# A lightweight convolution and a SwiGLU block: half of one DMA placing issued later on ScalarE, two values ahead of two taps on VectorE

## The chip, the cores and the metric

One core of a Trainium2 chip runs the whole program. Its engines are TensorE (PE in the profile, with its weight loads as PEld), VectorE (DVE), ScalarE (ACT), GpSimd (POOL) and SyncE (SP, which here only issues DMAs). Each engine works off its own list of instructions in the order in which the program gave them, and waits on semaphores for the others. The metric is the device time of one execution in microseconds (us), lower is better.

## What is computed

The reference, cut to what matters (B = 8, S = 4096, D = 192, 8 heads, 7 taps, 32768 tokens in all, inner width 1536, all in fp32):

```python
w = softmax(weight, axis=-1)                     # 8 heads x 7 taps
x_pad = concatenate([zeros((B, 6, D)), x], axis=1)
out = einsum('hk,bskhg->bshg', w, x_unf)         # causal convolution, 7 taps, weights by head
x = out.reshape(B * S, D)

rms = sqrt(mean(x * x, axis=-1) + 1e-06)
xn = x / rms * rms_g
g = xn @ w_gate
val = xn @ w_val
return (g * sigmoid(g) * val) @ w_out
```

## The kernel before, in words

The tokens are cut into 32 pieces of 1,024, which the code calls pairs (two groups of 512 tokens each). For every pair the kernel

- loads x with its halo into `xh` (`load_heads`, issue L144, eight DMAs on SP),
- convolves it into `y` (`tap` L421 in whole, or `part_tap` in three parts of 512 columns: the first tap on ACT into a PSUM bank at L437, the other six on DVE at L445, the last of which writes `y`),
- normalises: `square` on ACT (L461), `reduce` on DVE (L472 to L474), `factor` on POOL (L478 to L484), `spread` on DVE (L491), `scale` on POOL (L499), which leaves `yn`,
- turns the result over through DRAM: `place` writes `yn` to the scratch `xd` (L635, one DMA for each of eight heads), `fetch` reads it back as `xb`, features on partitions (L648, four DMAs; `fetch_part`, L661, in later pairs),
- multiplies with the gate and value weights, and then with the output weights.

From the second pair on the products go by a scheme with fewer multiplications (Strassen-like): it needs sums of operands, which DVE makes at L670 from `xb` into `xc` (`x_sum`), and sums of weights, which POOL makes at L346 and L350 (`w_sums`) and L825 (`out_sums`). Its products on PE are L759, its output products L899.

The first pair is plain: products at L1011 (24 groups of six, in an upper and a lower half of the array), a silu on ACT at L1021 and the value product on DVE at L1028 for each group, then the output products at L1051 (`outer`), cleared from PSUM by ACT at L1059 and DVE at L1063 and stored at L1068. While it runs, the weights are converted (L287 to L319, L298 to L302, L310, L311), the second pair (p = 1) is convolved and normalised, and the third (p = 2) is begun, with its x loaded early.

There are eight PSUM banks, ps0 to ps3 for one half and ps4 to ps7 for the other. A list of free banks is kept for each half while the program is written. The part taps of pair 2 take ps1, ps5 and ps3; the second half of `outer` for the first pair starts in ps1, once the part taps have given it back.

The order is written by hand. For the first pair the string `START` has a letter for each step, and each letter calls the next step of one generator: `p` a group of products, `s` its silu, `v` its value product, `c` a tap of pair 1, `w` four sums of weights, `i` and `o` steps of conversion, `n` a step of normalising, `t` the placing of pair 1. The list `LATER` puts more steps at places (numbers on a line of dues, `put(at, ...)`), and the code behind it puts the part taps, the fetch and the sums the same way. Steps with smaller numbers are emitted first:

```python
put(c + 240 + 700 * (j // 2), functools.partial(part_tap, 2, 0, j))
later(place(2), c + 2450)
```

with `base` = 4 x 1509 and `c` = `base + 200`. So the first two L437 of pair 2 (j = 0, 1) stand at `base + 440`, the fetch of pair 1 at `base + 450`, the third L437 (j = 2) at `base + 1140`. The step `t` stands at `base + 60` in `LATER`; in this kernel it issues all eight DMAs of L635, the odd heads on ACT, the even ones on SP. From pair 2 on `place` issues all eight on SP.

Of the kernel before, what the change touches and what calls it, by code (L numbers as in the profile page):

```python
# [19 lines left out]
def kernel(  # L20
# [10 lines left out]
    nc = tc.nc  # L31
# [3 lines left out]
    H, K = weight.shape  # L35
# [201 lines left out]
    def load_out(i):  # L237
# [28 lines left out]
        out=taps[:], in0=w_sb[:], in1=stat[:].to_broadcast([P, H, K]), op=ALU.subtract  # L266
# [7 lines left out]
        out=taps[:], in0=taps[:], in1=ssum[:].to_broadcast([P, H, K]), op=ALU.mult  # L274
# [84 lines left out]
    def convert_in(u):  # L359

        t = raw.pop(("in", u))
        dst = wf[u][:, 0:9, :].rearrange("p (k f) n -> p k (f n)", k=KP)
        step = P if u == 0 else NF * P
        parts = [slice(i, i + step) for i in range(0, NF * P, step)]
        return [
            convert(t[:, :, c, :], exp_i[:, :, c], mf_i[:, :, c], dst[:, :, c], rg_sb)
            for c in parts
        ]

    def convert_out(i):  # L370
        dst = wo_sb[:, i * PF : (i + 1) * PF, :]
        yield from convert(raw.pop(("out", i)), *cvt[i % 3], dst)
# [131 lines left out]
    def conv(p):  # L504

        for k in range(K):
            tap(p, k)
            if k == K - 1:
                load(p + 1)
            yield  # L510

    def norm(p):
        for part in (square, reduce, factor, spread, scale):
            part(p)
            yield
# [107 lines left out]
    def place(p):  # L623

        if p >= PAIRS:
            return
        y = yn.pop(p)  # L630
        xd = scr[p] = dram.tile([D, PT], F32, name="xd")
        to = xd[:].rearrange("(h a) (b t) -> h b a t", a=GS, t=TB)
        for h in range(H):
            q = nc.scalar if p == 1 and h % 2 else nc.sync
            q.dma_start(out=to[h], in_=y[h::H])  # L635
        yield

    def x_op(i):
        return xb[:, i // KP, i % KP, :] if i < 2 * KP else xc[:, i - 2 * KP, :]
# [36 lines left out]
    def bank(half, i):  # L676
        return ps[half * 4 + i]
# [6 lines left out]
    def pick(h, full):  # L684

        i = next((i for i in free[h] if ((h, i) in whole) == full), free[h][0])
        free[h].remove(i)
        return i
# [5 lines left out]
    def put(at, do):  # L694
        heapq.heappush(line, (at, next(tick), do))
# [301 lines left out]
    def plain(hts):  # L997


        groups = [(u, g, f) for u in range(NU) for g in (1, 0) for f in range(NF)]  # L1000
        groups[0 : 2 * NF] = [(0, g, f) for f in range(NF) for g in (1, 0)]
        held = {}

        def products():
            for u, g, f in groups:
                if len(hts) <= u:
                    hts.append(big.tile([P, 2, NF, T], F32, name="ht"))
                bks = held[u, g, f] = [free[h].pop(0) for h in range(2)]
                for k in range(KP):
                    for h in range(2):  # L1010
                        nc.tensor.matmul(  # L1011
                            out=bank(h, bks[h])[:], lhsT=wf[u][HALF[h], k * NF + f, :],
                            rhs=xb[HALF[h], g, k, :], start=(k == 0), stop=(k == KP - 1),
                            skip_group_check=True,
                        )
                yield

        def silus():
            for i in groups:
                sg = tiles.pop(0)  # L1020
                nc.scalar.activation(out=sg[:], in_=bank(0, held[i][0])[:], func=AF.Silu)  # L1021
                held[i].append(sg)
                yield

        def values():
            for u, g, f in groups:
                *bks, sg = held.pop((u, g, f))
                nc.vector.tensor_tensor(  # L1028
                    out=hts[u][:, g, f, :], in0=bank(1, bks[1])[:], in1=sg[:], op=ALU.mult
                )  # L1030
                tiles.append(sg)
                for h in range(2):
                    free[h].append(bks[h])
                yield

        return products(), silus(), values()
# [7 lines left out]
    def outer(p, hts, base):  # L1044


        def mm(h, bks, g, j, w, f, first, give=None):
            if first:
                bks[h] = free[h].pop(0) if first is True else pick(h, False)
                whole.discard((h, bks[h]))  # L1050
            nc.tensor.matmul(  # L1051
                out=bank(h, bks[h])[:, w : w + D],
                lhsT=hts[f // NF][HALF[h], g, f % NF, j * P : (j + 1) * P],
                rhs=wo_sb[HALF[h], f, :], start=(f == 0 and w == 0),
                stop=(f == FC - 1), skip_group_check=True,
            )

        def low(dst, bks, n):
            nc.scalar.copy(out=dst, in_=bank(0, bks[0])[:, 0:n])  # L1059
            free[0].append(bks[0])  # L1060

        def upp(dst, bks, n):
            nc.vector.tensor_tensor(out=dst, in0=bank(1, bks[1])[:, 0:n], in1=dst, op=ALU.add)  # L1063
            free[1].append(bks[1])

        def store(g, o_sb, lo=0, hi=T // P):
            r = p * PT + g * T
            nc.sync.dma_start(  # L1068
                out=out[r + lo * P : r + hi * P, :].rearrange("(j p) d -> p j d", p=P),
                in_=o_sb[:, lo:hi, :],  # L1070
            )

        def soon(*a):
            put(base + n * STEP + LAG + OVER + 1, functools.partial(store, *a))

        n = 0

        def mms(bks, g, j, w, fs, first):
            nonlocal n
            for i, f in enumerate(fs):  # L1080
                for h in range(2):
                    at = base + n * STEP + h * LAG
                    put(at, functools.partial(mm, h, bks, g, j, w, f, first if i == 0 else False))
                n += 1

        def evac(dst, bks, w):
            put(base + n * STEP + OVER, functools.partial(low, dst, bks, w))
            put(base + n * STEP + LAG + OVER, functools.partial(upp, dst, bks, w))

        for g in range(2):  # L1090
            o_sb = outs.tile([P, T // P, D], F32, name="o_sb")
            if g == 0:

                bks = [{}, {}]
                for fs in (range(0, FC // 2), range(FC // 2, FC - NF)):
                    for j in range(4):
                        mms(bks[j // 2], g, j, j % 2 * D, fs, j % 2 == 0 and fs[0] == 0)
                for j in range(4):
                    mms(bks[j // 2], g, j, j % 2 * D, range(FC - NF, FC), False)
                    if j % 2:  # L1100
                        dst = o_sb[:, j - 1 : j + 1, :].rearrange("p j d -> p (j d)")
                        evac(dst, bks[j // 2], 2 * D)
            else:
                for j in range(0, 2 if p == PAIRS - 1 else 4, 2):
                    b = {}
                    mms(b, g, j, 0, range(FC), "used" if j else True)
                    mms(b, g, j + 1, D, range(FC), False)
                    evac(o_sb[:, j : j + 2, :].rearrange("p j d -> p (j d)"), b, 2 * D)

                if p == PAIRS - 1:  # L1110
                    soon(g, o_sb, 0, 2)
                    for j in range(2, 4):
                        b = {}
                        mms(b, g, j, 0, range(FC), True)
                        evac(o_sb[:, j, :], b, D)
                        soon(g, o_sb, j, j + 1)
                    continue
            soon(g, o_sb)
# [7 lines left out]
    def done(it):  # L1126
# [7 lines left out]


    START = (
        "XxxxxxXDdDdDTDdadTbTaTfbTakTakTakTkbkKkKkKkbkbfpoffpfsicpsvivOpsipisvicpsvpvwsicwpvs"
        "iwpvscwpsiwvpisvicpsvovpwispvswcipvwspsiwOvpsiwvipsvvpswopsvcpsvOnovoOpsonvOpsnoOvnopsoO"
    )
    LATER = (  # L1140
        (30, "s"), (35, "v"), (40, "O"), (45, "v"), (50, "O"), (55, "n"), (60, "t"),
# [9 lines left out]
    for i in range(2, NO):  # L1151
        load_out(i)
    hts = []
    p, sl, v = plain(hts)
    pieces = {
        **cross(),
        **dict(zip("abf", convert_in(0))),
        "i": itertools.chain(*[convert_in(u)[0] for u in range(1, NU)]),
        "o": itertools.chain(*[convert_out(i) for i in range(0, NO, 2)]),
        "O": itertools.chain(*[convert_out(i) for i in range(1, NO, 2)]),  # L1160
        "c": conv(1), "n": norm(1), "t": place(1),
        "p": p, "s": sl, "v": v,
        "w": itertools.chain(*[w_sums(u) for u in range(NU)]),
# [15 lines left out]

    base = NU * SPAN  # L1180
    put(base - 1, lambda: outer(0, hts, base))
    put(base + 450, functools.partial(fetch, 1))
    both.extend(flat[:, i * T : (i + 1) * T] for i in range(NK - len(both)))
    rest.extend(t[:, 2, :] for t in tl6)
# [69 lines left out]
```

## Time and profile before

| what | value |
|---|---|
| device time, three runs | 2611.20, 2612.31, 2613.34 us, median 2612.31 |
| the profiled execution | 2610.37 us, its span 2608.6 us |
| granted TensorE clock over the span | 0.998 |
| PE busy | 2572.9 us, 99% |
| DVE, POOL, ACT busy | 89%, 84%, 59% |
| PE's share of the chain that ended last | 96% |
| L759, products of the later pairs | 62% of that chain |
| L899, output products of the later pairs | 33% |
| L1011 and L1051, the first pair | 1% each |

The span runs from the first to the last instruction; the execution's own time is 1.8 us more. The page divides the span into 40 slices of 65 us; in those a stall of a few us can't be seen, so stages are read from timelines over short stretches. A timeline line has the start, the length, the engine, the line, what is written and read, and how many instructions are merged in it; a bracket at its end has the idle time of the engine ahead of it and what ended it.

### The profile page before, as it was taken

Reading aid. Unit: us, or ns where it says so; the run is one execution under the profiler, and the core shown is the slowest. Engines: PE = TensorE matmul, PEld = TensorE weight load, DVE = VectorE, ACT = ScalarE, POOL = GpSimd, SP = SyncE. Lnnn points to the kernel's source line nnn. Section 1 sums busy time; section 2 is a strip of 40 time slices with the busy share of each in tenths; the row PEclk is TensorE's granted clock in tenths of the full one; section 3 lists DMA queues with packets and bytes.
Section 4 is the critical chain, followed back from the end, with each engine's and each line's share of the span. In section 5 each row is a group of like instructions: output and inputs, shape, how many; then the busy total and the mean of one; then the engine's idle time right before and its main releaser. Section 6 shows DMA issues by size and latency. Waiting matters only on the chain.

```text
span 2608.6 us, 60634 instructions
## 1 busy us (share of the span) xinstructions
PE 2572.9 (99%) x23794; PEld 1756.9 (67%) x23794; DVE 2309.3 (89%) x3679; ACT 1545.0 (59%) x2812; POOL 2189.0 (84%) x1786
## 2 busy tenths in 40 slices
PE   6899999999999999999999999999999999999999
PEld 3586667666676666676666766666766666766666
DVE  8888989889989889898899898898898898988975
ACT  5365556765556655557655566555576555676554
POOL 3878889888898888898888988888988888988877
PEclk9999999999999999999999999999999999999999
DMA  6222331223322223313233222233132333222210
GB/s 144 51 39 56 63 54 41 54 41 63 63 45 49 44 52 63 60 38 58 34 63 63 47 48 45 51 63 63 40 55 34 62 63 54 41 54 41 50 44 13
DMA packets 512602, 137.35 MB, mean 53 GB/s; under 512 B 484284, under 2 KB 486844, under 8 KB 512189
## 3 DMA queue, kind: packets, MB, share of 16 engines
q1 hardware_dynamic: 509068, 132.80, 26.9%
q8 instruction: 186, 3.05, 0.5%
q10 hardware_dynamic: 3248, 0.69, 0.1%
q14 instruction: 100, 0.82, 0.1%
HBM read 83.87 MB, written 49.55 MB: 51 GB/s over the span
## 4 chain that ended last, share of the span: by engine, by line
PE 96%; DVE 2%; issue 0%; DMA 0%; ACT 0%; POOL 0%; ACTq 0%; DVEq 0%; SPq 0%; POOLq 0%
PE ps L759 62%; PE ps L899 33%; PE ps L1011 1%; PE ps L1051 1%; DMA x<-in_x_dram 0%; DVE ht L1028 0%; DVE xc L304 0%; DVE y L406 0%; DVE y L421 0%; DVE ps L445 0%; DVE y L394 0%; DVE wf L319 0%; ACT xb L615 0%; PE ps L595 0%; ACTq L635 0%
## 5 line engine op out<-in xcount | busy, mean ns | idle before, releaser
L759 PE MATMUL ps<-xc,wf 64*128 64x512 f32 x4960 | 1216.6, 591 | 0.0
L759 PEld LDWEIGHTS ps<-xc,wf 64*128 64x128 f32 x4960 | 680.5, 186 | 376.8 <-issue 181.3
L759 PE MATMUL ps<-xb,wf 64*128 64x512 f32 x2480 | 682.3, 591 | 0.0
L708 ACT ACTIVATE tile<-ps 128x512 f32<-128x512 f32 x678 | 391.2, 593 | 389.7 <-PE ps L759 296.1
L708 ACT ACTIVATE tls<-ps 128x512 f32<-128x512 f32 (+1 forms) x562 | 323.4, 589 | 437.9 <-PE ps L759 221.4
L811 POOL TENSOR_TENSOR ht<-ht,tile 128x512 f32<-128x512 f32 x329 | 419.0, 1275 | 144.2 <-ACT tile L804 65.6
L759 PEld LDWEIGHTS ps<-xb,wf 64*128 64x128 f32 x2480 | 354.0, 187 | 183.0 <-issue 96.3
L811 POOL TENSOR_TENSOR ht<-ht,tls 128x512 f32<-128x512 f32 x260 | 330.6, 1274 | 86.2 <-ACT tls L804 40.4
L708 ACT ACTIVATE ps<-ps 128x512 f32<-128x512 f32 (+1 forms) x589 | 336.1, 581 | 88.0 <-PE ps L899 32.6
L927 POOL TENSOR_TENSOR early<-ht 128x512 f32<-128x512 f32 x279 | 354.9, 1277 | 5.1 <-POOL ht L811 0.3
L445 DVE SCALAR_TENSOR_TENSOR ps<-xh,tp,ps 128x512 f32<-128x512 f32 x450 | 320.3, 748 | 10.7 <-ACT ps L437 8.5
L899 PE MATMUL ps<-ht,wo_sb 128*32 128x128 f32 (+2 forms) x5208 | 318.5, 380 | 0.0
L899 PEld LDWEIGHTS ps<-ht,wo_sb 128*32 128x32 f32 x5208 | 233.9, 110 | 81.7 <-POOL ht L811 23.5
L899 PE MATMUL ps<-ht,x 128*32 128x128 f32 (+2 forms) x4464 | 250.7, 379 | 0.0
L791 DVE TENSOR_TENSOR tile<-ps,tile 128x512 f32<-128x512 f32 x349 | 237.4, 683 | 10.4 <-PE ps L759 5.4
L927 POOL TENSOR_TENSOR ht<-ht 128x512 f32<-128x512 f32 x186 | 239.1, 1286 | 4.9
L791 DVE TENSOR_TENSOR ht<-ps,tile 128x512 f32<-128x512 f32 x328 | 222.5, 680 | 5.9 <-ACT tile L708 5.9
L899 PEld LDWEIGHTS ps<-ht,x 128*32 128x32 f32 x4464 | 184.6, 110 | 61.2
L804 ACT ACTIVATE tile<-tile 128x512 f32<-128x512 f32 x349 | 214.5, 625 | 0.0
L791 DVE TENSOR_TENSOR ht<-ps,tls 128x512 f32<-128x512 f32 x292 | 198.9, 681 | 7.1 <-ACT tls L708 3.9
L791 DVE TENSOR_TENSOR tls<-ps,tls 128x512 f32<-128x512 f32 x271 | 184.8, 683 | 16.7 <-PE ps L759 13.3
L899 PE MATMUL ps<-early,x 128*32 128x256 f32 (+2 forms) x3348 | 196.0, 379 | 0.0
(130 smaller groups left out, 3250.8 us busy)
## 6 DMA issues: line engine op xcount, KB each, us to landing
xb<-xd SPq DMA_DIRECT2D x124, 384.0 KB
xd<-yn SPq DMA_DIRECT2D x244, 96.0 KB
xh<-in_x_dram SPq DMA_DIRECT2D x192, 105.0 KB
out_dram<-o_sb SPq DMA_DIRECT2D x122, 96.0 KB
out_dram<-o_sb SPq DMA_DIRECT2D x62, 128.0 KB
xh<-in_x_dram SPq DMA_DIRECT2D x56, 98.4 KB
out_dram<-o_sb SPq DMA_DIRECT2D x122, 32.0 KB
ht<-in_moe_w_gate_dram SPq DMA_DIRECT2D x12, 192.0 KB
```

The source lines that it names most:

```text
L445: nc.vector.scalar_tensor_tensor(out=dst, in0=xk, scalar=w, in1=at, op0=ALU.mult, op1=ALU.add)
L708: nc.scalar.activation(out=dst, in_=src, func=AF.Copy, scale=float(s))
L759: nc.tensor.matmul(out=self.new(v, h, True) if first else self.old(v, h), lhsT=wf[self.u][HALF[h], WAT[i], :], rhs=x_op(XOP[i])[HALF[h]], ...
L791: nc.vector.tensor_tensor(out=self.hv(v) if h else t[:], in0=self.old(v, h), in1=t[:], op=plus(s))
L804: nc.scalar.activation(out=t[:], in_=src[:], func=AF.Silu)
L811: engine[eng].tensor_tensor(out=self.hv(v), in0=src, in1=t[:], op=ALU.mult)
L899: nc.tensor.matmul(out=self.bank(b)[i * Q : (i + 1) * Q, at : at + n], lhsT=left, rhs=cols, start=fresh, stop=True, skip_group_check=True, ...
L927: engine[eng].tensor_tensor(out=dst, in0=a, in1=b, op=op)
L1011: nc.tensor.matmul(out=bank(h, bks[h])[:], lhsT=wf[u][HALF[h], k * NF + f, :], rhs=xb[HALF[h], g, k, :], start=(k == 0), stop=(k == KP - 1 ...
L1051: nc.tensor.matmul(out=bank(h, bks[h])[:, w : w + D], lhsT=hts[f // NF][HALF[h], g, f % NF, j * P : (j + 1) * P], rhs=wo_sb[HALF[h], f, :] ...
```

## The change

Three edits.

1. `place` becomes a generator of two steps for p = 1: the first issues the even heads on SP, the second the odd heads on ACT. For every other pair it stays one step with all heads on SP.
2. The second step is put at `base + 445`: behind the first two L437 of pair 2 (`base + 440`) and ahead of the fetch of pair 1 (`base + 450`). The first step stays at `base + 60`.
3. In `START`, twice, a `v` that stood behind a `c` now stands ahead of it (`wsicw` becomes `wsivcw` with the `v` behind it gone, and the same once more in the next row).

```diff
-        for h in range(H):
-            q = nc.scalar if p == 1 and h % 2 else nc.sync
-            q.dma_start(out=to[h], in_=y[h::H])
-        yield
+        for first in range(2) if p == 1 else (0,):
+            q = nc.scalar if first else nc.sync
+            for h in range(first, H, 2 if p == 1 else 1):
+                q.dma_start(out=to[h], in_=y[h::H])
+            yield
...
     START = (
-        "XxxxxxXDdDdDTDdadTbTaTfbTakTakTakTkbkKkKkKkbkbfpoffpfsicpsvivOpsipisvicpsvpvwsicwpvs"
-        "iwpvscwpsiwvpisvicpsvovpwispvswcipvwspsiwOvpsiwvipsvvpswopsvcpsvOnovoOpsonvOpsnoOvnopsoO"
+        "XxxxxxXDdDdDTDdadTbTaTfbTakTakTakTkbkKkKkKkbkbfpoffpfsicpsvivOpsipisvicpsvpvwsivcwps"
+        "iwpvscwpsiwvpisvivcpsovpwispvswcipvwspsiwOvpsiwvipsvvpswopsvcpsvOnovoOpsonvOpsnoOvnopsoO"
     )
...
     put(base - 1, lambda: outer(0, hts, base))
+    put(base + 445, functools.partial(next, pieces["t"], None))
     put(base + 450, functools.partial(fetch, 1))
```

In the instruction lists this moves the following and nothing else. On ACT, the four issues of L635 go from ahead of the three L437 of pair 2 to between the second and the third. On DVE, a value product L1028 changes places with the tap L421 ahead of it, at two points: those at 59.20 and at 70.37 us in the profile before. The lists of PE, POOL and SP are the same, but for the numbers of the DMA semaphores that some of them wait for.

## The prediction

> **What bounds the kernel now.** I read the page first: PE is busy 99% of the span and holds 96% of the chain that ended last. So an edit is worth only what PE waits, or loses in speed, because of it. The 40 slices show PE below 9 in the first two alone, so I went through 0 to 150 us: the timelines of PE, ACT, DVE, POOL and SP, then a table of stretches for the granted clock.
>
> PE, 100.5 to 142 us (start, us, what; in brackets the idle time before it and its releaser):
>
> ```profile
> 101.10 15.70 PE L1051 MATMUL ps<-wo_sb,ht 64*128 64x192 f32 x183
> 123.57 18.39 PE L1051 MATMUL ps<-wo_sb,ht 64*128 64x192 f32 x195 [6.77 <-DVE y L445]
> 141.64 0.69 PE L759 MATMUL ps<-xc,wf 64*128 64x512 f32 x1
> ```
>
> The largest hole in PE's work, 6.77 us, ends with a tap of pair 2 (L445), which frees ps1. Who holds the taps up, ACT and DVE:
>
> ```profile
> 105.62 0.54 ACT L302 ACTIVATE tls<-tls 128x384 f32<-128x384 uint32 x1
> 111.67 3.59 ACTq L635 DMA_DIRECT2D xd<-yn  x4
> 115.46 1.91 ACT L437 ACTIVATE ps<-xh,tp 128x512 f32<-128x512 f32 x3 [9.30 <-DMA xd<-yn]
> ```
>
> ```profile
> 106.27 1.39 DVE L304 SCALAR_TENSOR_TENSOR xc<-tls,xc 128x384 uint32<-128x384 uint32 x1
> 116.18 6.68 DVE L445 SCALAR_TENSOR_TENSOR ps<-xh,tp,ps 128x512 f32<-128x512 f32 x10 [8.52 <-ACT ps L437]
> 122.77 1.40 DVE L445 SCALAR_TENSOR_TENSOR y<-xh,tp,ps 128x512 f32<-128x512 f32 x2
> 124.09 3.91 DVE L445 SCALAR_TENSOR_TENSOR ps<-xh,tp,ps 128x512 f32<-128x512 f32 x5
> ```
>
> ACT has nothing to do from 106.16 to 111.67: the four issues of L635 stand first and wait for yn. The chain of waits confirms it and names the origin, POOL's scaling at L499:
>
> ```profile
> 108.76 2.87 POOL yn L499
> 111.63 0.36 POOL wf L350
> 111.99 0.27 ACTq L635
> ```
>
> The clock (columns: stretch, length, busy time and count of PE, PEld, DVE, ACT, POOL, PEclk, DMA share, GB/s):
>
> ```profile
> 116.80:123.50 6.70, 0.00 (x0) 0.00 (x0) 6.70 (x12) 0.98 (x2) 6.01 (x14) 0.81 0.61 141
> 123.50:125.50 2.00, 1.93 (x12) 1.93 (x14) 1.97 (x4) 0.00 (x0) 1.84 (x5) 0.50 1.07 214
> 127.50:129.50 2.00, 2.00 (x26) 2.00 (x26) 1.72 (x3) 0.68 (x1) 0.94 (x2) 0.94 0.00 1
> ```
>
> After the hole PE works at half clock until 127.74 (clock record of the trace). Two more small holes lie in the first pair's products, both before DVE's values (L1028):
>
> ```profile
> 61.87 1.13 PE L1011 MATMUL ps<-xb,wf 64*128 64x512 f32 x4 [0.24 <-DVE ht L1028]
> 73.03 1.55 PE L1011 MATMUL ps<-xb,wf 64*128 64x512 f32 x5 [0.22 <-DVE ht L1028]
> ```
>
> **What the Trainium skill says.** "TensorE: Matmul & The Clock Gate", Part 1: after an idle window of about 3.4 us the array falls to half clock, and an equally long busy window restores it. The trace agrees: 0.50 granted from 120.91 (4.1 us into the hole) to 127.74, 6.83 us. The same page, under "Architectural detail", calls ACT and DVE strict first-in first-out; the 9.30 us in which ACT's L437 stands behind the waiting issues is that. "DMA: Bandwidth & Descriptors", "Queues, rings and completion order": on one queue each DMA engine consumes descriptors in ring order. The trace agrees: the x loads (96-byte packets) issued at 221.69, behind output stores (256-byte packets), send their first packet at 222.5, as the stores' last ones leave. "SBUF — State Buffer", "SBUF: two separate sides": DVE and GpSimd share a port pair by an exclusive lock, which a DVE operation with two SBUF inputs takes part in. The taps of L445 have one input in PSUM, and L499 took 2.87 to 2.92 us in all 31 pairs beside a DVE that is 89% busy: no contention seen for this pair of operations.
>
> **Part 1, the placing.** The four DMA issues on ACT go behind the first two of the three L437; they still wait for L499. SP's four, and everything else on SP, POOL and PE, keep their order; only ACT's list changes.
>
> - When can the two L437 run? x of pair 2 (SP's issues from 90.09 to 96.98) has its last packet at 99.77. ps1 and ps5 were last read before 101. ACT is free at 106.16: two of 0.70 us at a pitch of 0.64 end at 107.5.
> - DVE ends its last L304 at 107.66 and then starts the taps, at 107.7 instead of 116.18: 8.5 us earlier. The first y ended 7.34 us after the first tap (123.52 less 116.18); now 115.05. It also needs L499 past (111.63), which it is.
> - The issues stay at 111.67 to 115.26, so the third L437 runs 115.4 to 116.1. The twelve taps end at about 115.7, the last six (4.7 us) at 120.85.
> - PE got to the end of its queue at 116.5. The bank is free at 115.05, so the hole closes. Start to start it was 123.569 - 116.475 = 7.09 where 0.16 is normal: 6.93 us.
> - With no hole the clock stays up. From 123.57 to 127.74 PE started 26 records 0.160 us apart against 0.080 at full clock: 26 x 0.080 = 2.08 us.
>
> **Part 2, two values ahead of taps.** L1028 of 0.68 us goes before a tap of L421 of 2.0 us, at 59.20 and at 70.37. Their silus ended at 53.64 and 64.56, so no new wait. ps5 comes free 1.9 us earlier, both holes vanish. Start to start they show 0.83 and 0.81 us for 0.43, and 0.53 for 0.43 on the next: 0.5 us each, 1.0 in all. The taps follow at once, and the second value stays where it was. Next late are the values at 65.59 and 76.03: they end 0.1 to 0.2 us before PE, now 0.5 to 1.0 ahead, needs their banks. So between 0.7 and 1.0; I take 0.9.
>
> **What is late next.** PE alone would gain 6.93 + 2.08 + 0.9 = 9.9 us at its first L759 (141.64, so 131.7). But that needs an x sum (xc slot 5), and this chain does not move: L499 ends 111.63, the placing lands (last packet 117.78), SP fetches xb:
>
> ```profile
> 118.25 2.60 SPq L648 DMA_DIRECT2D xb<-xd  x4
> 128.87 7.30 SPq L144 DMA_DIRECT2D xh<-in_x_dram  x8
> ```
>
> The last 2,048-byte packet of xb ends at 127.63. DVE starts the sums at 127.7 (in between: square 120.9 to 122.4, L472 to L474 done by 125, so DVE waits for xb). Before, the sums ran 132.58 to 140.56 and slot 5, the seventh, was there 5.44 us after their start: now 133.15. So PE waits 1.5 us at the first L759 (too short for the clock to fall) and starts it 8.5 us earlier. In the old trace three records of L1051 stood mixed into its start; free of them PE is up to 8.9 ahead.
>
> DVE, however, ends its sums at 135.7 and the two L1063 at 136.9; the values it owes PE's first bank (L785, 144.59 before) are due at 135.7. It is late by about 1.2 us, and PE has 0.7 us of room before the same bank's next product: 0.5 back. POOL's L499 and eleven L825 end at 144.9, its first L811 is due at 143.7; the idle 1.52 and 1.44 us before the next two take that up.
>
> The x load of pair 3 moves too: its eight issues follow DVE's last tap, now from 120.9 instead of 128.87, beside xb's packets. By ring order it goes behind them: nothing, at worst 0.5.
>
> Sum at the start of pair 1: 8.5 to 8.9, less 0.5: 8.2 us, within 7.2 to 9.0. From there PE is the bound (99%) and every stage follows it, so the shift reaches the end. The profiled execution took 2610.37 (span 2608.6 and 1.8 around it), 1.9 below the median of 2612.31. I take the gain off the median: 2604.1; the profiled span would be 2600.4.
>
> **Rivals.**
> - A, as above: 2604.1, own range 2602.8 to 2605.6. For it: the hole's releaser is named by the profile and every step has a measured duration. 74%.
> - B, the sums come later: packets of pair 3's x mix into xb's, or sums and L825 block each other more. If half of the DMA time from 122.2 on went to x, xb's remaining 5.4 us would take 10.8, to 133: gain 8.2 - 5.4 = 2.8, so 2609.5; a little mixing 2607. Against: the order of packets at 222. 12%.
> - C, the change doesn't do what it says: L437 or the first tap waits for something else ending near 115. Then the swaps alone, 0.9 us: 2611.4. Against: no engine shows unfinished work on ps1, ps5 or xh after 107.7. 9%.
> - D, slower: x of pair 3 goes wholly ahead of xb. xb then lands near 127.6 + 7.9 = 135.5, L759 starts at 141.0, and PE, idle for 9 us, comes back at half clock for 4 to 7 us: 2 to 3.5 lost. Gain 0.6 less that: 1.4 to 2.9 slower, 2614.5, and as much as 2618 if the late sums keep DVE behind for a second window. It decides from xb landing after 134.5. 5%, over 0.2% slower in 3%.
>
> **How the numbers follow.** What can be told from no change is 0.2%, 5.2 us. A lies wholly beyond it; of B about a third does. Faster 0.74 + 0.04 = 0.78; slower 0.03; the same 0.19. The range: A's, widened to half of B above: 2602.3 to 2607.5, which leaves about two in ten out.
>
> **What would show it.** L437 twice at 106.2 and the taps from 107.7; PE without idle time from 101 to 131.7 and clock 1.00 through 116 to 142; no idle before L1011 at 61 and 72; the issues of L635 still at 111.7; first x sum at 127.7; first L759 near 133.2 after an idle time of 1 to 2 us released by the x sums. It would be wrong if PE still idled near 116, if xb landed after 129, or if the lead at 142 shrank during the first pairs.

## The result and the profile after

| | device time, median | runs |
|---|---|---|
| before | 2611.81 us (2610.22 to 2615.09) | 22 |
| changed | 2607.56 us (2605.50 to 2609.83) | 22 |

The ratio is 0.9983, with a 95% interval of 0.9977 to 0.9990: 4.25 us or 0.17% faster. The direction is as forecast, the size about half: 8.2 us was forecast, and the median lies at the upper end of the range (2607.5), 0.06 us past it.

Lines from L635 on stand one higher in the changed kernel (L1011 is L1012, L635 L636, L648 L649, L670 L671, L759 L760, L1051 L1052, L1063 L1064). PE's timeline of the changed kernel, 100 to 142 us:

```profile
101.30 5.36 PE L1052 MATMUL ps<-wo_sb,ht 64*128 64x192 f32 x56
106.99 27.57 PE L1052 MATMUL ps<-wo_sb,ht 64*128 64x192 f32 x328 [0.33 <-DVE ht L1029]
136.21 4.00 PE L760 MATMUL ps<-xc,wf 64*128 64x512 f32 x7 [1.66 <-DVE xc L671]
```

The hole of 6.77 us is gone: after a wait of 0.33 us for the last values (L1029) the first pair's output products run through from 106.99 to 134.56. What made it is gone with it, as ACT's and DVE's timelines show:

```profile
107.24 1.28 ACT L437 ACTIVATE ps<-xh,tp 128x512 f32<-128x512 f32 x2
112.90 3.58 ACTq L636 DMA_DIRECT2D xd<-yn  x4
116.53 0.69 ACT L437 ACTIVATE ps<-xh,tp 128x512 f32<-128x512 f32 x1 [8.01 <-POOL wf L350]
```

```profile
108.77 6.67 DVE L445 SCALAR_TENSOR_TENSOR ps<-xh,tp,ps 128x512 f32<-128x512 f32 x10
115.35 1.39 DVE L445 SCALAR_TENSOR_TENSOR y<-xh,tp,ps 128x512 f32<-128x512 f32 x2
...
130.81 0.69 DVE L671 TENSOR_TENSOR xc<-xb 128x512 f32<-128x512 f32 x1 [5.01 <-DMA xb<-xd]
```

The first two L437 stand ahead of the issues, and the taps follow at once. But the third line of PE and the last of DVE show a new wait: PE idles 1.66 us for the x sums of pair 1, and these wait 5.01 us for `xb`. SP and the clock add to it. SP's timeline, and the table of stretches (stretch, length, busy time and count of PE, PEld, DVE, ACT, POOL, granted clock, DMA share, GB/s):

```profile
119.47 2.61 SPq L649 DMA_DIRECT2D xb<-xd  x4
122.18 12.34 SPq L144 DMA_DIRECT2D xh<-in_x_dram  x8
```

```profile
133.00:136.40 3.40, 1.74 (x14) 1.47 (x12) 3.33 (x6) 0.48 (x1) 0.00 (x0) 1.00 1.03 142
136.40:139.80 3.40, 3.40 (x8) 1.39 (x9) 3.26 (x7) 1.08 (x2) 0.92 (x1) 0.50 0.26 88
```

The x load of pair 3 now follows the fetch at once and takes 12.34 us to issue instead of 7.30; what makes the issuing longer no run shows. And the clock falls to half just as pair 1's products begin, for 3.41 us, though PE had been busy for 1.74 of the 3.40 us before.

To compare executions I count from the first product of the first pair, since what lies ahead of it differs from run to run by 1 to 3 us (it came at 37.29 us in the profile before, at 38.57 here) and no edit touches it. "Pair 1's first" is the start of pair 1's first product (L759, L760 in the changed kernel), "24 records" the time from there to the start of the 24th following record of that line, "end" the start of PE's last matmul. Each row is one traced execution:

| us from the first product | pair 1's first | 24 records | end | less than before |
|---|---|---|---|---|
| before | 104.35 | 5.50 | 2565.47 | |
| changed | 97.64 | 7.41 | 2560.73 | 4.74 |

At pair 1's first product the changed kernel is 6.71 us ahead; the next 24 records give 1.91 back, which leaves 4.80; from there to the end both are alike (4.74 us at the end). So all of the difference arises between 100 and 145 us, and the question is what took 9.0 us (the hole's 6.93 and the clock's 2.08) down to 4.7.

### The profile page after: what moved, and what is told of

The parts are those of the page before. It is cut to its first block, busy times and chain, and to the rows that moved or that the text cites. A ratio compares the mean times of both kernels' runs of the same rounds, so it can differ in the third digit from the quotient of the medians.

```text
span 2605.1 us, 60636 instructions
## 1 busy us (share of the span) xinstructions
PE 2573.1 (99%) x23794; PEld 1761.3 (68%) x23794; DVE 2308.5 (89%) x3679; ACT 1544.9 (59%) x2812; POOL 2188.0 (84%) x1786
## 4 chain that ended last, share of the span: by engine, by line
PE 96%; DVE 2%; DMA 1%; issue 0%; ACT 0%; SPq 0%; POOL 0%; ACTq 0%; DVEq 0%; POOLq 0%
PE ps L760 62%; PE ps L900 33%; PE ps L1012 1%; DMA x<-in_x_dram 0%; DMA xb<-xd 0%; DVE ht L1029 0%; DVE y L421 0%; DVE y L406 0%; DVE xc L304 0%; DVE y L394 0%; PE ps L595 0%; DVE wf L319 0%; DVE xc L671 0%; ACT xb L615 0%; DMA xd<-yn 0%
## 5 line engine op out<-in xcount | busy, mean ns | idle before, releaser
L760 PE MATMUL ps<-xc,wf 64*128 64x512 f32 x4960 | 1219.3, 592 | 1.7 <-DVE xc L671 1.7
L760 PEld LDWEIGHTS ps<-xc,wf 64*128 64x128 f32 x4960 | 682.4, 186 | 379.2 <-issue 184.9
L760 PE MATMUL ps<-xb,wf 64*128 64x512 f32 x2480 | 683.3, 591 | 0.0
L760 PEld LDWEIGHTS ps<-xb,wf 64*128 64x128 f32 x2480 | 355.3, 187 | 182.2 <-issue 96.9
```

The lines of the kernel that those rows point to most:

```text
L760: nc.tensor.matmul(out=self.new(v, h, True) if first else self.old(v, h), lhsT=wf[self.u][HALF[h], WAT[i], :], rhs=x_op(XOP[i])[HALF[h]], ...
```

## The experiments

Each kernel was timed against the kernel before on the same chip, the first four on one chip, the next three on another, the last on a third. The 95% intervals of the ratios are 0.07% to 0.13% (2 to 3 us) wide to either side, so where two of these kernels differ by less, the argument rests on their traces.

**The swaps alone.** `START` of the changed kernel, all else as before.

```diff
-        "XxxxxxXDdDdDTDdadTbTaTfbTakTakTakTkbkKkKkKkbkbfpoffpfsicpsvivOpsipisvicpsvpvwsicwpvs"
-        "iwpvscwpsiwvpisvicpsvovpwispvswcipvwspsiwOvpsiwvipsvvpswopsvcpsvOnovoOpsonvOpsnoOvnopsoO"
+        "XxxxxxXDdDdDTDdadTbTaTfbTakTakTakTkbkKkKkKkbkbfpoffpfsicpsvivOpsipisvicpsvpvwsivcwps"
+        "iwpvscwpsiwvpisvivcpsovpwispvswcipvwspsiwOvpsiwvipsvvpswopsvcpsvOnovoOpsonvOpsnoOvnopsoO"
```

> Only the two swaps in START; the placing as before. Theory 1 (the swaps shorten PE's work list by about 0.6 us, but what releases PE in the hole near 116 us is ACT and DVE behind L499, which don't move): the hole grows by what the swaps save, time equal to before within 0.5 us. Rival (the swaps are worth 0.5 us or more by themselves, as the forecast had it): 0.5 to 1.0 us under before.

Measured: 2612.06 against 2611.68 us, ratio 1.0000 (0.9992 to 1.0009): no gain, though the interval alone would leave room for 0.9 us. PE's output products began 62.88 us after the first product instead of 63.32. They then waited 0.32 us for the last values, and the hole stayed as long as it was; it did not grow, as had been expected, since the saving was waited away ahead of it:

```profile
106.95 10.99 PE L1051 MATMUL ps<-wo_sb,ht 64*128 64x192 f32 x130 [0.32 <-DVE ht L1028]
124.71 19.00 PE L1051 MATMUL ps<-wo_sb,ht 64*128 64x192 f32 x195 [6.76 <-DVE y L445]
```

**The placing alone.** `START` as before, the other two edits kept.

```diff
-        "XxxxxxXDdDdDTDdadTbTaTfbTakTakTakTkbkKkKkKkbkbfpoffpfsicpsvivOpsipisvicpsvpvwsivcwps"
-        "iwpvscwpsiwvpisvivcpsovpwispvswcipvwspsiwOvpsiwvipsvvpswopsvcpsvOnovoOpsonvOpsnoOvnopsoO"
+        "XxxxxxXDdDdDTDdadTbTaTfbTakTakTakTkbkKkKkKkbkbfpoffpfsicpsvivOpsipisvicpsvpvwsicwpvs"
+        "iwpvscwpsiwvpisvicpsvovpwispvswcipvwspsiwOvpsiwvipsvvpswopsvcpsvOnovoOpsonvOpsnoOvnopsoO"
```

> Only the placing in two steps; START as before. Theory 1 (pair 1's first product waits for the x sums and these for xb, so what PE gains ahead of that is waited away): equal to the changed kernel within 0.7 us, about 4.2 us under before, with PE idle about 1 us instead of 1.66 ahead of the first product of pair 1. Rival (the swaps carry part of the gain): about 0.6 to 1.0 us above the changed kernel.

Measured: 2607.56 us, ratio 0.9984 (0.9977 to 0.9991), the same median as the changed kernel. The whole gain is the placing's. The detail was off: PE idled 1.67 us in front of pair 1, not 1, because the sums of that execution came late too:

```profile
136.63 4.26 PE L760 MATMUL ps<-xc,wf 64*128 64x512 f32 x7 [1.67 <-DVE xc L671]
```

**The x load of pair 3 later.** The changed kernel, with

```diff
-    put(c + 1500, functools.partial(load, 3))
+    put(c + 1800, functools.partial(load, 3))
```

> The changed kernel with the x load of pair 3 moved behind the first store of the output (L1069) on SP, so that it can't be issued before xb has landed and the first sums are made. Theory A (the earlier load mixes with the end of xb: in the changed kernel the sums started 1.27 us after xb's last packet and 1.9 us later than L499's chain would give; and the late start made the clock fall): sums start within 0.1 us of xb's last packet and about 1.9 us earlier against the placing's issue, 1.9 us gained if the clock still falls, up to 3.6 us if it doesn't. Rival (xb's end is set by the fetch itself, or what was lost was lost after the sums): sums start as in the changed kernel, time within 0.7 us of it.

Measured: 2605.13 us, ratio 0.9974 (0.9964 to 0.9985), 2.4 us under the changed kernel's median. From its SP timeline (the fetch, and behind it an output's store instead of the load), and its DVE timeline (the first sum, the last one, and the clearing of two banks behind it):

```profile
118.38 2.60 SPq L649 DMA_DIRECT2D xb<-xd  x4
130.55 0.42 SPq L1069 DMA_DIRECT2D out_dram<-o_sb  x1
```

```profile
128.64 0.69 DVE L671 TENSOR_TENSOR xc<-xb 128x512 f32<-128x512 f32 x1 [3.90 <-DMA xb<-xd]
...
135.93 0.68 DVE L671 TENSOR_TENSOR xc<-xb,xc 128x512 f32<-128x512 f32 x1
...
136.69 0.98 DVE L1064 TENSOR_TENSOR o_sb<-ps,o_sb 128x384 f32<-128x384 f32 x2
```

From the first issue of the fetch to the first sum it is 10.26 us here and 11.34 in the changed kernel: 1.1 us, not the 1.9 expected. Half of the wait behind the last packet stayed (0.57 us of 1.27), so I had counted part of the fetch's own tail as mixing. Theory A holds in kind: the load's 96-byte packets start at 127.78 in the changed kernel, `xb`'s last 2,048-byte packet ends at 129.54, and the sum starts 1.27 us after that. With the load away the clock stays at 1.00, so what is gained holds the clock's part too; the two are not separated here. But PE's timeline shows a wait that I had not foreseen:

```profile
134.23 1.95 PE L760 MATMUL ps<-xc,wf 64*128 64x512 f32 x6 [0.68 <-DVE xc L671]
137.26 0.69 PE L760 MATMUL ps<-xc,wf 64*128 64x512 f32 x1 [1.09 <-DVE o_sb L1064]
```

Pair 1's second product goes to ps7, which holds an output of the first pair until L1064 clears it, and that L1064 stands behind all eleven sums in DVE's list. In the changed kernel the half clock covers this wait: the second product starts at 139.25 there, 0.06 us after that L1064 has ended, and no idle time shows ahead of it.

**Two matmuls as a filler.** The changed kernel, with work that keeps PE busy while it waits for the sums:

```diff
     emit(float("inf"))
+    for _ in range(2):
+        nc.tensor.matmul(
+            out=ps[5][:], lhsT=wf[0][:, 0, :], rhs=hts[0][:, 0, 0, :], start=True, stop=True,
+            skip_group_check=True,
+        )
```

> The changed kernel with two matmuls more (fp32, 128x512, into the free bank ps5, which nobody reads) between the last output product of the first pair and the first product of pair 1; their result is not used. Theory B (PE's idle 1.66 us made the clock fall to half for 3.41 us at the start of pair 1, which cost about 1.7 us): clock stays 1.00 from 34 us on, 1.0 to 1.7 us under the changed kernel. Rival (in that stretch PE waits for the x sums anyway, so the clock costs nothing, or the filler is in the way): the same time or up to 0.5 us above it.

Measured: 2606.28 us, ratio 0.9979 (0.9970 to 0.9987), 1.3 us under the changed kernel's median. The table of stretches, for the same stretches as above:

```profile
133.00:136.40 3.40, 3.40 (x14) 1.93 (x14) 3.33 (x6) 0.48 (x1) 0.00 (x0) 1.00 1.14 189
136.40:139.80 3.40, 2.81 (x12) 1.18 (x10) 2.67 (x6) 1.08 (x2) 1.50 (x1) 1.00 0.07 22
```

PE gets no operand earlier (pair 1's first product at 97.87, against 97.64), and still the 24 records take 6.67 us instead of 7.41: theory B. That it is less than 1.7 us has its reason in the same L1064, for which PE now waits 0.59 us. The granted clock over the span also differs between executions of one kernel, and the time with it. Of the 22 of the changed kernel, eleven have 0.997 and a median of 2608.88 us, the other eleven 0.998 or 0.999 and a median of 2606.38; the traced one is of these. With the filler all eleven have 0.998 or more. How much of that arises here, and how much at the start of an execution (half clock for 3.41 or 6.83 us in the traces), is not told apart; but it can explain why the medians differ by 1.3 us and the ends of the two traces by 0.54.

**The clearing ahead of the sums.** As with the later load, and the sums emitted behind the second and third L1064; stores and load behind the last.

```diff
-    xat = [c + i for i in (1660, 1730, 2060, 2130, 2200, 2270, 2290)]
-    xat += [c + i for i in (2360, 2370, 2380, 2390)]
+    xat = [c + 2700 + 10 * i for i in range(11)]
...
-    later(norm(2), c + 1510, c + 1600, c + 2310, c + 2420, c + 2440)
-    later(place(2), c + 2450)
+    later(norm(2), c + 1510, c + 1600, c + 2310, c + 2900, c + 2910)
+    later(place(2), c + 2920)
...
-        put(base + n * STEP + LAG + OVER + 1, functools.partial(store, *a))
+        put(base + 3790, functools.partial(store, *a))
...
-    put(c + 1800, functools.partial(load, 3))
+    put(base + 3792, functools.partial(load, 3))
```

> The run before with the later load, and in it the eleven x sums behind the clearing of the second and third bank pair of the first pair's output (L1064) in DVE's list; both stores (L1069) and the x load of pair 3 go behind the last clearing. Theory C (with the load out of the way, pair 1's second product waits for ps7, whose clearing stood behind all eleven sums): first product of pair 1 about 0.7 us earlier against the placing, the 1.09 us idle ahead of the second gone, a shorter one left at the third (ps4, cleared behind the sums); 1.0 to 2.0 us under the run with the later load. Rival (the sums alone set the start): at most 0.7 us under it.

Measured: 2607.13 us, ratio 0.9981 (0.9973 to 0.9989). Each against its own kernel before, that is 5.5 us faster where the run with the later load was 6.6 us faster, and the traces say the same (5.34 and 6.41): no gain, and rather a loss, where theory C had promised 1 us or more. Its timelines of PE (the new wait), DVE (one of the sums) and POOL (what ran beside that sum):

```profile
139.88 0.69 PE L760 MATMUL ps<-xb,wf 64*128 64x512 f32 x1 [1.54 <-DVE o_sb L1064]
```

```profile
138.16 1.07 DVE L671 TENSOR_TENSOR xc<-xb,xc 128x512 f32<-128x512 f32 x1
```

```profile
135.65 3.03 POOL L826 TENSOR_TENSOR x<-wo_sb,x 128x192 f32<-128x192 f32 x3
```

The wait for ps7 is gone; the one for ps4, whose L1064 is still behind the sums, took its place and is longer. For the move had also put nine of POOL's L826 ahead of its L499, where the run with the later load has one, and most of them ran beside the sums: where two such operations overlap both are slower, a sum 1.07 us instead of 0.69, an L826 1.0 instead of 0.56, and from the first sum to the end of their L491 it took 9.7 us, against 8.1 with the later load. That is the likely reason why the move won nothing; the rest of theory C needed the next run.

**The sums split.** As the one before, with

```diff
-    xat = [c + 2700 + 10 * i for i in range(11)]
-    for i, at in zip((0, 1, 7, 2, 3, 5, 6, 10, 8, 9, 4), xat):
+    xat = [c + 2700 + 10 * i for i in range(7)] + [base + 3800 + 10 * i for i in range(4)]
+    for i, at in zip((3, 6, 0, 2, 1, 5, 10, 8, 9, 4, 7), xat):
...
-    later(norm(2), c + 1510, c + 1600, c + 2310, c + 2900, c + 2910)
-    later(place(2), c + 2920)
+    later(norm(2), c + 1510, c + 1600, c + 2310, base + 3850, base + 3860)
+    later(place(2), base + 3870)
```

> As the run with the clearing ahead, but the sums in the order in which pair 1's products ask for them, and the last four of them behind the clearing of ps4. Theory C: PE passes from the first pair's outputs to pair 1's products with no idle time over 0.3 us and at full clock; 0.5 to 1.5 us under the run with the clearing ahead, about 2604.0 to 2603.0 in all, since nothing is then left between the hole and the steady part. Rival (a later wait, DVE's or POOL's in pair 1, is behind it): no more than 0.3 us under it.

Measured: 2604.71 us, ratio 0.9970 (0.9959 to 0.9982), 2.4 us under the one before, on the same chip, and more than theory C had set. PE passes from one pair to the other without a pause, pair 1's first product at 95.31. Then, six us later, a wait that the theory did not have:

```profile
134.48 0.69 PE L760 MATMUL ps<-xc,wf 64*128 64x512 f32 x1
...
140.43 2.15 PE L760 MATMUL ps<-xc,wf 64*128 64x512 f32 x7 [0.86 <-DVE tile L786]
```

**The same without the swaps.** `START` as before.

> The run with the sums split, with START as in the kernel before (no swaps). If the swaps were worthless in the change only because PE waited for the sums afterwards, they must show here, where it doesn't: 0.5 to 0.8 us above the run with the sums split. Rival (what they save is given back at the last values of the first pair, L1029): within 0.3 us of it.

Measured: 2604.68 us, ratio 0.9969 (0.9957 to 0.9982), the same as with them, in time and (within 0.12 us) in the trace. The output products begin at 63.49 instead of 62.88 us, but then take 31.95 us to pair 1 instead of 32.44: of 0.61 us, 0.49 is given back, most of it at the last values (L1029). The rival is right: the swaps are worth 0.1 us where pair 1 doesn't wait for the sums.

**DVE first.** The sums split, with nine of them ahead of the clearing of ps4, and L826 behind L499.

```diff
-    xat = [c + 2700 + 10 * i for i in range(7)] + [base + 3800 + 10 * i for i in range(4)]
+    xat = [c + 2700 + 10 * i for i in range(9)] + [base + 3800 + 10 * i for i in range(2)]
...
-    later(out_sums(), *[base + 2600 + 60 * i for i in range(4 * NM)])
+    later(out_sums(), *[base + 3900 + 10 * i for i in range(4 * NM)])
```

> The run with the sums split, with nine sums instead of seven ahead of the clearing of ps4, and POOL's twelve L826 behind its scaling L499. Theory D (what the run with the sums split lost after its first products, 1.6 us between PE's 16th and 24th record of pair 1, is DVE's lateness: its two L786 began 2.3 us after PE was through with their banks, of which 1.42 us were DVE's wait for PE at ps4 and about 1.3 us sums lengthened beside POOL's L826): the L786 start about 1.5 to 2 us earlier against PE's first product, PE's wait for L786 falls from 0.86 us to under 0.3, records 16 to 24 take 2.0 to 2.5 us instead of 3.4, time 0.7 to 1.4 us under that run. Rival (POOL's late L826 hold up its L812 and PE later, or the wait sits elsewhere): the same within 0.4 us.

Measured: 2604.09 us against 2612.99, ratio 0.9966 (0.9954 to 0.9978), the fastest of all: 8.9 us under before, twice what the change brought. The two edits were made together, so their parts are not told apart. DVE's L786 now come 2.94 us after PE's first product (135.47) instead of 5.25:

```profile
136.38 0.56 DVE L1064 TENSOR_TENSOR o_sb<-ps,o_sb 128x384 f32<-128x384 f32 x1 [0.19 <-PE ps L1052]
136.85 1.28 DVE L671 TENSOR_TENSOR xc<-xb,xc 128x512 f32<-128x512 f32 x2
138.05 0.24 DVE L491 STREAM_TRANSPOSE s<-s 128x64 f32<-128x64 f32 x1
138.41 1.29 DVE L786 TENSOR_TENSOR tile<-ps,tile 128x512 f32<-128x512 f32 x2
```

All in one table:

| us from the first product | pair 1's first | 24 records | end | less than before |
|---|---|---|---|---|
| swaps alone | 104.99 | 5.50 | 2566.12 | -0.65 |
| placing alone | 97.91 | 9.16 | 2562.85 | 2.62 |
| filler | 97.87 | 6.67 | 2560.19 | 5.28 |
| load later | 96.66 | 7.14 | 2559.06 | 6.41 |
| clearing ahead | 96.94 | 7.60 | 2560.13 | 5.34 |
| sums split | 95.31 | 7.08 | 2558.31 | 7.16 |
| split, no swaps | 95.43 | 7.15 | 2558.43 | 7.04 |
| DVE first | 95.33 | 5.50 | 2556.62 | 8.85 |

The last row has the 5.50 us of the kernel before, and its gain is the 9.0 us of the hole and its clock, but for 0.2. So the account closes. Two rows need a word. In the execution traced with the placing alone the half clock lasted 6.83 us, twice as long as in the changed kernel's, hence its 9.16; their medians agree. With the swaps alone it lasted until 5.4 us after the hole, where in the kernel before it was 4.2, and 1.2 us more at half speed make 0.6 of the 0.65.

## Why the prediction was right and where it was wrong

- The hole. Right: L437 ahead of the issues, taps at once, no idle time near 116, no half clock behind it. Its two terms, 6.93 and 2.08 us, are confirmed in their sum by the last run, in which nothing takes their place: pair 1 comes 9.0 us earlier there.
- Cases and chances. The likeliest case, 2604.1, did not come; the time is that of the mild form of rival B ("a little mixing 2607"), but the mixing makes only a part of what is missing, and B named neither the clock nor ps7. So it is in part luck that the median lies as near to the range as it does. "Faster by over 0.2%" had 0.78; 0.17% was measured. Of the signs of being wrong one came, the lead that shrank (6.71 to 4.80 us, at pair 1's first 24 records), and a second in part: the first sum, which waits for `xb`, starts at 129.53 if one counts as in the kernel before (130.81 less 1.28), past the 129 of the forecast.
- The swaps. Wrong: 0.9 us in the sum, nothing measured. Both small holes vanished as said, but the values at the end of the first pair hardly come earlier, so PE waits for those instead (0.33 us), and where nothing follows that could hide a gain, 0.1 us is left.
- "The x load of pair 3 ... By ring order it goes behind them: nothing, at worst 0.5." This term was mis-sized: with the load later the sums came 1.1 us earlier and PE's end, the clock's part included, 1.7 (6.41 against 4.74). What the Trainium skill says of ring order ("DMA: Bandwidth & Descriptors", "Queues, rings and completion order") was no ground for a term of nothing: the same section says that the order holds on each DMA engine by itself, and in the trace the first 96-byte packet starts 1.76 us before the last 2,048-byte one ends. The "sums at 127.7" had a second gap: even with the load later they start 0.57 us after the last packet, where the forecast allowed 0.07.
- "PE waits 1.5 us at the first L759 (too short for the clock to fall)." The wait was right (1.66), the bracket wrong. The Trainium skill, "TensorE: Matmul & The Clock Gate", Part 1, speaks of an idle window of about 3.4 us; here a stretch of 3.4 us in which PE was busy for half of the time sufficed. The filler puts 1.3 us on it.
- "DVE ... is late by about 1.2 us, and PE has 0.7 us of room ...: 0.5 back." This step named the wrong instruction first. DVE's lateness reaches PE through the clearing of ps7 at the second product (1.09 us with the later load) before it does through L786, and when the clearing and the sums are out of the way, L786 costs 1.6 us (records of the split run) where 0.5 was set.

So the mechanism and its place were right, and the failure is in the paragraph on what is late next and in the swaps. All that is late behind the hole took 4.1 us (8.85 less 4.74), where the forecast had allowed 1.7 (9.9 less 8.2): the load, the clock and DVE's lateness, each written off at 0 to 0.5 us, stood one behind the other, each in part covered by the one before. The swaps' 0.8 us are most of the rest.

## What to carry to other kernels

When a stall goes, every engine's list behind it must be walked down to the next PE instruction that waits, bank by bank, not just to the one operand that seems last: here it was a transfer, then a bank's clearing behind eleven sums, then two evacuations. An engine that idles on a late operand should have the clearings of the old stage ahead of that operand in its list; here that paid only once the operations that it pushed together were parted again. A transfer that an edit lets start earlier belongs in the sum as a cost, if a critical one is in flight on the same queue.

## What the runs showed of the hardware

- The granted clock fell to 0.50 after a stretch with PE busy for 1.74 of 3.40 us (1.73 with the placing alone). In the run with the clearing ahead, with idle times of 0.94 and 1.54 us, 3 us apart, it stayed at 1.00, though PE was busy for only 1.87 of the 3.41 us up to 139.88.
- In all ten traces the granted clock changes only at whole multiples of 3.41 us from its first change. Between 100 and 150 us it stayed at 0.50 for one such step in the changed kernel, two in the kernel before and with the placing alone, three with the swaps alone. In three of these four it rose behind the first of them through which PE was busy; why it took one more with the placing alone stays open.
- The first sum that waited for the fetch started 1.24 to 1.32 us after the fetch's last data packet had ended where the x load was on the queue behind it (three traces), and 0.54 to 0.57 us after it where it was not (five).
- A sum of two SBUF operands on DVE and one on POOL at the same time both took longer: 1.07 for 0.69 us, and 1.0 for 0.56 (run with the clearing ahead).
